# Attention steps spread by weight among the feed-forward steps, from the second H group on

## The chip, the cores and the metric

The kernel runs on one core of one Trainium2 chip. The time is device microseconds of one execution; smaller is better.

## The reference

Two stages, one after the other, over 8 batches of 576 tokens with 8 heads of 64:

```python
scores = scale * np.matmul(q, k.transpose(0, 1, 3, 2))
bias = slopes[:, None, None] * (-np.abs(rel))[None]      # rel = i - j
mask = (rel >= 0) & (rel < 128)
attn = softmax(np.where(mask, scores + bias, -1e9))
x = (attn @ v), heads side by side                       # 4608 x 512
h = x @ w_in                                             # 512 -> 2048
g = h * (1.0 / (1.0 + np.exp(-beta * h)))
out = g @ w_out                                          # 2048 -> 512
```

A row looks back over 128 columns at most, so a block of 128 rows needs its own block of keys and the one before.

## The kernel before

All matmuls are in bf16 with sums in f32. The work is a set of small steps, each a function that issues its instructions on several engines at once.

Attention, for each batch `b`. `TP(b, p)` transposes q and k of head pair `p` on TensorE (eight transposes into two PSUM tiles of `psum_t`, two VectorE copies into `QK`, L230); `TT(b)` does the last 64 rows. Batches from `NTE` = 3 on are transposed by DMA instead (`TD`, L249, on SyncE's queue SP), after a cast on GpSimd (POOL, L129). `SC(b, m, p)` makes scores of a head pair for half the key blocks in one tile of `psum_s`, which has one buffer; for batches 0 and 1 the bias table is added by a matmul and ScalarE takes one exponential (L285), for the later ones ScalarE takes four with a bias (L290) and VectorE multiplies by a mask (L294). `PV(b, qb, g)` multiplies four heads of a row block with the values `VS` (L317, L321) and normalizes on VectorE (L326, L327) into `xn`. `X(b, qb)` transposes `xn` into `XT`: for batches 0 to 2 on TensorE with a copy (L350), for later ones by DMA from SP (L341).

Feed-forward, for each group `g` of 512 tokens (9 groups). `HS(g, j)`, called H below, is four 512-column matmuls (L362), a tanh on ScalarE (`sig`, L367) and a VectorE operation (`gT`, L368); 16 per group. Its PSUM tiles come from `psum_h` (two buffers), in groups 0 and 1 also from `psum_o` (two). `OS(g, i, n)`, called O, is four matmuls (L378); every fourth is followed by a ScalarE evacuation (L384) and, later, a store from POOL.

The order on TensorE is the order in which the program calls the steps. `spread(moe, todo, lead, tail)` walks over the list `moe` of H and O steps and calls after each its share of the attention steps in `todo`, counted by number: none after the first `lead`, all of them before the last `tail`. `merge` puts the loads (`load_qk`, `load_v`), casts, `TD` and the DMA form of `X` (`lazy`) among the steps at due times counted in steps. `by_pair` is the list of a batch that is transposed on TensorE, `by_block` that of a later one.

Before, the stages run so: batch 0 alone; then hs(0), 16 H, with batch 1 spread among them (`lead` 3, `tail` 0); hs(1), 16 H, bare; os(0) and half of os(1), 24 O, with all of batch 2; group 2: hs(2) with the other half of os(1) as H H O eight times, with batch 3 up to the rows that group 3 needs; groups 3 to 8: H of `g` and O of `g - 1` by turns, with the batches' rest; then 16 bare O.

POOL's own queue issues, in an order that the scheduler sets for the early part and the program for the later: the casts of the loaded f32 tiles (`fst`, 13 buffers) of q, k (L113, L119) and v (L141), the loads of W1 and W2, which cast on the way, and from batch 2 on the values (L136), which also cast on the way into `VS`.

## Time and profile before

| | |
|---|---|
| median of 11 runs | 350.56 us (347.57 to 353.08) |
| the profiled execution | 352.3 us, of which its span 350.5 |
| mean granted TensorE clock | 0.984 |
| busy share | TensorE 93%, ScalarE 60%, VectorE 56%, POOL 30% |
| DMA | 138495 packets, 47.67 MB, 125649 of them under 512 B |

A busy share covers stages with quite different limits, so the stages are read one by one: hs(0) with batch 1 runs from 25.6 to 63.3 us, hs(1) from there to 77 us, the 24 O with batch 2 to 109.8 us, group 2 to about 138 us, and the last bare steps from 300 us on. "PEclk" is the clock that TensorE was granted, as a share of full speed. In the views, a releaser behind "<-" is what ended a wait.

### The profile page before, as it was taken

Reading aid. Unit: us, or ns where it says so; the run is one execution under the profiler, and the core shown is the slowest. Engines: PE = TensorE matmul, PEld = TensorE weight load, DVE = VectorE, ACT = ScalarE, POOL = GpSimd, SP = SyncE. Lnnn points to the kernel's source line nnn. Section 1 sums busy time; section 2 is a strip of 40 time slices with the busy share of each in tenths; the row PEclk is TensorE's granted clock in tenths of the full one; section 3 lists DMA queues with packets and bytes.
Section 4 is the critical chain, followed back from the end, with each engine's and each line's share of the span. In section 5 each row is a group of like instructions: output and inputs, shape, how many; then the busy total and the mean of one; then the engine's idle time right before and its main releaser. Section 6 shows DMA issues by size and latency. Waiting matters only on the chain.

```text
span 350.5 us, 6171 instructions
## 1 busy us (share of the span) xinstructions
PE 327.1 (93%) x2279; PEld 154.2 (44%) x2279; DVE 196.9 (56%) x421; ACT 210.9 (60%) x407; POOL 106.8 (30%) x173
## 2 busy tenths in 40 slices
PE   6988969898999789999999999999999999999995
PEld 2454424444454344344454445444544445444442
DVE  6477726776663776566466655665666465334400
ACT  4655843575734895577568756776588654544411
POOL 7639346111574341323225332532000000100000
PEclk9899988999999999999999999999999999999999
DMA  7999999960999999999649995993123002010021
GB/s 206 228 177 251 167 239 232 211 134 21 176 200 178 218 172 167 174 163 153 138 95 177 181 189 138 198 183 68 45 68 61 31 32 67 30 62 30 30 86 66
DMA packets 138495, 47.67 MB, mean 136 GB/s; under 512 B 125649, under 2 KB 135905, under 8 KB 138465
## 3 DMA queue, kind: packets, MB, share of 16 engines
q1 hardware_dynamic: 103520, 31.15, 49.5%
q0 software_dynamic: 34912, 16.13, 34.5%
q8 instruction: 18, 0.29, 0.4%
q14 instruction: 13, 0.10, 0.1%
q10 hardware_dynamic: 32, 0.01, 0.0%
HBM read 36.71 MB, written 9.44 MB: 132 GB/s over the span
## 4 chain that ended last, share of the span: by engine, by line
PE 61%; DMA 13%; issue 9%; ACT 5%; POOL 4%; DVE 4%; SPq 2%; POOLq 0%
PE ops L378 28%; PE hps L362 25%; DMA fst<-in_v_dram 5%; DMA fst<-in_q_dram 4%; ACT pt L290 3%; PE sps L277 3%; PE pv L321 2%; POOL vs L136 2%; DMA fst<-in_k_dram 2%; DMA W<-in_moe_w_in_dram 2%; PE pv L317 2%; SPq L109 1%; DVE gT L368 1%; ACT sig L367 1%; POOL bst L129 1%
## 5 line engine op out<-in xcount | busy, mean ns | idle before, releaser
L367 ACT ACTIVATE sig<-hps,beta_h 128x512 bf16<-128x512 f32 x144 | 99.4, 692 | 80.9 <-PE hps L362 76.6
L362 PE MATMUL hps<-XT,W 128*128 128x512 bf16 x576 | 146.2, 383 | 1.0 <-DVE gT L368 1.0
L378 PE MATMUL ops<-W,gT 128*128 128x512 bf16 x576 | 144.8, 379 | 0.0
L368 DVE SCALAR_TENSOR_TENSOR gT<-sig,hps 128x512 bf16<-128x512 bf16 x144 | 98.3, 684 | 69.5 <-ACT sig L367 69.2
L290 ACT ACTIVATE pt<-sps,bias 128x256 bf16<-128x256 f32 (+1 forms) x192 | 75.1, 479 | 11.9 <-PE sps L277 11.8
L362 PEld LDWEIGHTS <-W 128*128 128x128 bf16 x576 | 52.4, 98 | 60.0 <-issue 4.8
L378 PEld LDWEIGHTS <-gT 128*128 128x128 bf16 x576 | 52.2, 98 | 57.4 <-issue 1.7
L389 POOL DMA_DIRECT2D out_dram<-osb x32 | 17.9, 559 | 171.1 <-ACT osb L384 171.1
L294 DVE TENSOR_TENSOR pt<-pt,mask 128x1024 bf16<-128x1024 bf16 x48 | 35.3, 736 | 24.1 <-ACT pt L290 24.1
L129 POOL CAST bst<-fst 128x512 bf16<-128x512 f32 (+1 forms) x50 | 31.3, 646 | 29.1 <-DMA fst<-in_q_dram 22.7
L384 ACT ACTIVATE osb<-ops 128x512 f32<-128x512 f32 x36 | 21.7, 603 | 26.3 <-PE ops L378 26.3
L327 DVE TENSOR_TENSOR xn<-pv,zs 128x256 bf16<-128x256 f32 (+1 forms) x80 | 33.6, 420 | 2.1
L321 PE MATMUL pv<-vs,pt 128*128 128x65 bf16 x320 | 29.6, 196 | 5.4 <-POOL vs L141 3.3
L326 DVE RECIPROCAL zs<-pv 128x4 f32<-128x4 f32 (+1 forms) x80 | 14.1, 177 | 29.8 <-PE pv L321 29.0
L277 PE MATMUL sps<-qkT 64*128 64x256 bf16 (+2 forms) x320 | 25.6, 255 | 3.8 <-ACT pt L290 3.8
L321 PEld LDWEIGHTS <-pt 128*128 128x128 bf16 x320 | 22.2, 99 | 12.8 <-DVE pt L294 2.7
L317 PE MATMUL pv<-vs,pt 128*128 128x65 bf16 x256 | 24.8, 195 | 1.7 <-DVE xn L327 1.0
L136 POOL DMA_DIRECT2D vs<-in_v_dram x30 | 25.5, 853 | 0.5 <-PE pv L321 0.4
L317 PEld LDWEIGHTS <-pt 128*128 128x128 bf16 x256 | 20.2, 99 | 12.4 <-issue 4.5
L277 PEld LDWEIGHTS <-qkT 64*128 64x128 bf16 x320 | 11.2, 95 | 31.4 <-issue 30.0
L285 ACT ACTIVATE pt<-sps 128x1024 bf16<-128x1024 f32 x16 | 15.9, 1027 | 12.7 <-PE sps L277 12.2
L230 DVE COPY qkT<-tps 128x512 bf16<-128x512 bf16 x24 | 15.5, 684 | 4.0 <-PE tps L226 3.9
(45 smaller groups left out, 104.6 us busy)
## 6 DMA issues: line engine op xcount, KB each, us to landing
fst<-in_q_dram SPq DMA_DIRECT2D x32, 256.0 KB, 4.2
fst<-in_k_dram SPq DMA_DIRECT2D x32, 256.0 KB, 4.8
out_dram<-osb POOLq DMA_DIRECT2D x32, 256.0 KB, 2.8
vs<-in_v_dram POOLq DMA_DIRECT2D x24, 128.0 KB, 5.6
fst<-in_v_dram SPq DMA_DIRECT2D x8, 256.0 KB, 8.0
W<-in_moe_w_in_dram POOLq DMA_DIRECT2D x4, 512.0 KB, 7.7
W<-in_moe_w_out_dram POOLq DMA_DIRECT2D x4, 512.0 KB, 15.2
fst<-in_q_dram SPq DMA_DIRECT2D x8, 128.0 KB, 5.4
```

Of the source, the lines that this page charges most:

```text
L129: nc.gpsimd.tensor_copy(out=t[0 : ROWS[sb], i], in_=f)
L136: nc.gpsimd.dma_start(out=VS[b % 2][0 : ROWS[sb], sb, :, 0:D], in_=v[b, :, P * sb : P * sb + ROWS[sb], :].rearrange("h p d -> p h d"),)
L277: nc.tensor.matmul(o, lhsT=qk[64 * e : 64 * e + 64, 1, p, P * kb : P * kb + P], rhs=qk[64 * e : 64 * e + 64, 0, p, P * kb : P * kb + nq], ...
L290: nc.scalar.activation(out=pt[:, e, cols], in_=sps[:, e, cols], func=ACTF.Exp, scale=qscale, bias=bias[:, half, h : h + 1],)
L294: nc.vector.tensor_tensor(out=pt[:], in0=pt[:], in1=masks[m][:].rearrange("p (o c) -> p o c", o=1).broadcast_to([P, 2, 512]), op=ALU.mult,)
L317: nc.tensor.matmul(pv[:, hl, 0 : D + 1], lhsT=weights(b, qb - 1, h, 1), rhs=vs[:, qb - 1, h, 0 : D + 1], start=True, stop=False,)
L321: nc.tensor.matmul(pv[:, hl, 0 : D + 1], lhsT=weights(b, qb, h, 0), rhs=vs[:, qb, h, 0 : D + 1], start=qb == 0, stop=True,)
L327: nc.vector.tensor_tensor(out=xn[0:nq, 4 * g : 4 * g + 4, :], in0=pv[0:nq, :, 0:D], in1=zs[0:nq].broadcast_to([nq, 4, D]), op=ALU.mult,)
L362: nc.tensor.matmul(hps[:], lhsT=W1[:, c, bass.ts(j, P)], rhs=XT[:, c, c0 : c0 + TOKG], start=(c == 0), stop=(c == NDM - 1),)
L367: nc.scalar.activation(out=sig[:], in_=hps[:], func=ACTF.Tanh, scale=beta_h[:, j : j + 1])
L368: nc.vector.scalar_tensor_tensor(out=gts[g][:, j, :], in0=sig[:], scalar=1.0, in1=hps[:], op0=ALU.add, op1=ALU.mult)
L378: nc.tensor.matmul(ops_[:], lhsT=gT[:, j, i * P : i * P + P], rhs=W2[:, j, :], start=(j == 0), stop=(j == NFF - 1),)
```

## The change

1. `spread` counts by weight: an SC weighs 2, a PV, TP half, TT or TensorE X weighs 1, a DMA X nothing, and a step is called once its weight's share of the slots has passed.
2. `TP` is split in two halves (one PSUM tile each), which are separate steps.
3. hs(0) takes batch 1 without its last block (its two PV and its X), with `tail` 2. The rest of batch 1 and batch 2 up to block 2 are spread over hs(1), os(0) and half of os(1) as one list of 40 steps (`lead` 6, `tail` 7). What is left of batch 2's blocks 3 and 4 goes to the head of batch 3's list.
4. Batch 2's X goes by DMA from SP; batch 1's X is copied by ScalarE instead of VectorE.
5. The loads of batch 2's values are issued after W2's, not as early as the scheduler finds room.
6. Every group from 2 on has the form of the old group 2: H H O eight times with the second half of O of `g - 1`, and then, but for the last, the first half of its own O, eight in a row.
7. `by_block` and the due times in `merge` are altered by a step or two.

The queue of POOL around the loads of batch 2's values (`vs_72` of `in_v`; `vs_73` are batch 1's, `W_79` is W1, `W_80` is W2), before:

```order
L136 DMA vs_72<-in_v_dram 128x8x64
L119 CAST tail_77<-fst 64x512
L136 DMA vs_72<-in_v_dram 128x8x64
L113 CAST bst<-fst 128x512 x2
L136 DMA vs_72<-in_v_dram 128x8x64
L113 CAST bst<-fst 128x512 x2
L189 DMA W_79<-in_moe_w_in_dram 128x4x512
L141 CAST vs_73<-fst 128x8x64
L136 DMA vs_72<-in_v_dram 64x8x64
L141 CAST vs_73<-fst 128x8x64 x3
L192 DMA W_80<-in_moe_w_out_dram 128x4x512 x4
```

and now:

```order
L119 CAST tail_77<-fst 64x512 x2
L113 CAST bst<-fst 128x512 x4
L189 DMA W_79<-in_moe_w_in_dram 128x4x512
L141 CAST vs_73<-fst 128x8x64 x4
L192 DMA W_80<-in_moe_w_out_dram 128x4x512 x4
L141 CAST vs_73<-fst 64x8x64
L113 CAST bst<-fst 128x512 x4
L119 CAST tail_76<-fst 64x512 x2
L113 CAST bst<-fst 128x512 x3
L136 DMA vs_72<-in_v_dram 128x8x64
L113 CAST bst<-fst 128x512
L136 DMA vs_72<-in_v_dram 128x8x64 x3
```

Batch 2's five loads, which stood among the casts of batch 1 and ahead of W1's last part, stand behind W2's and behind casts of batch 2.

VectorE in hs(0), where batch 1's q and k are copied out of the TP tiles (`qkT<-tps`), before:

```order
L368 SCALAR_TENSOR_TENSOR gT<-sig,hps 128x512 x3
L230 COPY qkT_75<-tps 128x512
L368 SCALAR_TENSOR_TENSOR gT<-sig,hps 128x512
L230 COPY qkT_75<-tps 128x512 x3
L368 SCALAR_TENSOR_TENSOR gT<-sig,hps 128x512
L244 COPY qkT_75<-tps 128x8x64
L368 SCALAR_TENSOR_TENSOR gT<-sig,hps 128x512
L230 COPY qkT_75<-tps 128x512 x2
L368 SCALAR_TENSOR_TENSOR gT<-sig,hps 128x512
L230 COPY qkT_75<-tps 128x512 x2
```

and now:

```order
L366 SCALAR_TENSOR_TENSOR gT<-sig,hps 128x512 x3
L229 COPY qkT_75<-tps 128x512
L366 SCALAR_TENSOR_TENSOR gT<-sig,hps 128x512
L229 COPY qkT_75<-tps 128x512
L366 SCALAR_TENSOR_TENSOR gT<-sig,hps 128x512
L229 COPY qkT_75<-tps 128x512 x2
L243 COPY qkT_75<-tps 128x8x64
L366 SCALAR_TENSOR_TENSOR gT<-sig,hps 128x512
L229 COPY qkT_75<-tps 128x512
L366 SCALAR_TENSOR_TENSOR gT<-sig,hps 128x512
```

Three copies stood after one `gT`; now it is one, one, and two with TT's, and the later ones stand alone.

ScalarE at the start of group 2, where four `pt` of 256 (or 320, 192, 320, 192) are one SC and a `sig` is one H, before:

```order
L367 ACTIVATE sig<-hps,beta_h 128x512
L290 ACTIVATE pt<-sps,bias 128x256 x4
L367 ACTIVATE sig<-hps,beta_h 128x512
L290 ACTIVATE pt<-sps,bias 128x256 x8
L367 ACTIVATE sig<-hps,beta_h 128x512 x2
L290 ACTIVATE pt<-sps,bias 128x256 x4
L367 ACTIVATE sig<-hps,beta_h 128x512 x2
L290 ACTIVATE pt<-sps,bias 128x320
L290 ACTIVATE pt<-sps,bias 128x192
L290 ACTIVATE pt<-sps,bias 128x320
L290 ACTIVATE pt<-sps,bias 128x192
```

and now:

```order
L365 ACTIVATE sig<-hps,beta_h 128x512 x3
L289 ACTIVATE pt<-sps,bias 128x256 x4
L365 ACTIVATE sig<-hps,beta_h 128x512 x2
L289 ACTIVATE pt<-sps,bias 128x256 x4
L365 ACTIVATE sig<-hps,beta_h 128x512
L289 ACTIVATE pt<-sps,bias 128x256 x4
L365 ACTIVATE sig<-hps,beta_h 128x512 x2
L382 ACTIVATE osb<-ops 128x512
```

Five SC stood among six H before; now three stand among eight, and no two are neighbours.

The diff, cut to its core:

```diff
     def load_w2(n):
-        nc.gpsimd.dma_start(out=W2[:, bass.ts(n, 4), :], in_=W2v[:, bass.ts(n, 4), :])
+        return nc.gpsimd.dma_start(out=W2[:, bass.ts(n, 4), :], in_=W2v[:, bass.ts(n, 4), :])
...
-    def TP(b, p):
-        src = staged.pop((b, p))
-        for i in range(2):
+    def TP(b, p, i):
+        src = staged[b, p]
...
-        if b >= NTE:
+        if b >= NPE:
             for at, r0, r1 in parts:
                 nc.sync.dma_start_transpose(out=XT[:, :, at : at + r1 - r0], in_=xnv[r0:r1, :])
             return
...
-        copy = nc.vector.tensor_copy if b else nc.scalar.copy
         for at, r0, r1 in parts:
-            copy(out=XT[:, :, at : at + r1 - r0], in_=xt[:, :, r0:r1])
+            nc.scalar.copy(out=XT[:, :, at : at + r1 - r0], in_=xt[:, :, r0:r1])
...
+    cost = {}
+
     def spread(moe, todo, lead=0, tail=3):
-        done, n = 0, len(moe)
+        total, n = sum(cost.get(f, 0) for f in todo), len(moe) - lead - tail
+        done, k = 0, 0
         for i, it in enumerate(moe):
             flush()
             it()
-            to = len(todo) * (i + 1 - lead) // (n - lead - tail)
-            while done < min(len(todo), to):
-                todo[done]()
-                done += 1
+            while k < len(todo) and (i + 1 - lead >= n or (
+                done + cost.get(todo[k], 0)) * n <= total * (i + 1 - lead)):
+                done += cost.get(todo[k], 0)
+                todo[k]()
+                k += 1
+        for f in todo[k:]:
+            f()
+
+    def step(f, c):
+        cost[f] = c
+        return f
+
+    def tp(b, p, i):
+        return step(lambda: TP(b, p, i), 1)
+
+    def tt(b):
+        return step(lambda: TT(b), 1)
 
     def sc(b, m, p):
-        return lambda: SC(b, m, p)
+        return step(lambda: SC(b, m, p), 2)
 
     def pv(b, qb, g):
-        return lambda: PV(b, qb, g)
+        return step(lambda: PV(b, qb, g), 1)
 
     def x(b, qb):
-        f = lambda: X(b, qb)
+        f = step(lambda: X(b, qb), int(b < NPE))
         at[b, qb] = f
-        if b >= NTE:
+        if b >= NPE:
             lazy.append(f)
         return f
 
...
                 t0 = first[b] - 25 + 4.6 * sb
                 jobs.append((t0, lambda b=b, sb=sb, c=casts: c.append(load_qk(b, sb))))
-                jobs.append((t0 + 3.5, lambda c=casts: c.pop()()))
-                jobs.append((t0 + 6.5, lambda b=b, sb=sb: TD(b, sb)))
+                jobs.append((t0 + 4.5, lambda c=casts: c.pop()()))
+                jobs.append((t0 + 8.5, lambda b=b, sb=sb: TD(b, sb)))
                 jobs.append((first[b] - 16 + 3 * sb, lambda b=b, sb=sb: load_v(b, sb)))
         for i, f in enumerate(steps):
             if f in lazy:
-                jobs.append((i + 2.5, f))
+                jobs.append((i + 2, f))
         jobs.sort(key=lambda j: j[0])
         out = []
         for i, f in enumerate(steps):
...
 
     def by_pair(b):
         return [
-            lambda: TP(b, 0), lambda: TP(b, 1), sc(b, 0, 0), lambda: TT(b), sc(b, 0, 1),
-            lambda: TP(b, 2), sc(b, 1, 0), lambda: TP(b, 3), sc(b, 1, 1), pv(b, 0, 0), sc(b, 0, 2),
-            pv(b, 1, 0), sc(b, 1, 2), pv(b, 2, 0), sc(b, 0, 3), pv(b, 3, 0), sc(b, 1, 3),
-            pv(b, 4, 0), pv(b, 0, 1), pv(b, 1, 1), x(b, 0), pv(b, 2, 1), x(b, 1), pv(b, 3, 1),
-            x(b, 2), pv(b, 4, 1), x(b, 3), x(b, 4),
+            tp(b, 0, 0), tp(b, 0, 1), sc(b, 0, 0), tp(b, 1, 0), tp(b, 1, 1), tt(b), sc(b, 0, 1),
+            tp(b, 2, 0), sc(b, 1, 0), tp(b, 2, 1), sc(b, 1, 1), tp(b, 3, 0), pv(b, 0, 0),
+            tp(b, 3, 1), sc(b, 0, 2), pv(b, 1, 0), sc(b, 1, 2), pv(b, 2, 0), sc(b, 0, 3),
+            pv(b, 3, 0), sc(b, 1, 3), pv(b, 0, 1), pv(b, 1, 1), x(b, 0), pv(b, 2, 1), x(b, 1),
+            pv(b, 3, 1), x(b, 2), x(b, 3), pv(b, 4, 0), pv(b, 4, 1), x(b, 4),
         ]
 
     def by_block(b):
 
         e = b - 1
-        r = [pv(e, 2, 1), pv(e, 3, 1), x(e, 2), sc(b, 0, 0), x(e, 3), pv(e, 4, 1), sc(b, 0, 1),
-             x(e, 4)] if e >= NTE else [sc(b, 0, 0), sc(b, 0, 1)]
+        if e < NTE:
+            r = [sc(b, 0, 0), pv(e, 3, 1), x(e, 3), pv(e, 4, 0), sc(b, 0, 1), pv(e, 4, 1), x(e, 4)]
+        else:
+            r = [sc(b, 0, 0), pv(e, 2, 1), x(e, 2), pv(e, 3, 1), x(e, 3), sc(b, 0, 1),
+                 pv(e, 4, 1), x(e, 4)]
         return r + [
-            sc(b, 0, 2), pv(b, 0, 0), sc(b, 0, 3), pv(b, 1, 0),
-            pv(b, 0, 1), sc(b, 1, 0), x(b, 0), pv(b, 1, 1), sc(b, 1, 1), x(b, 1),
-            sc(b, 1, 2), pv(b, 2, 0), sc(b, 1, 3), pv(b, 3, 0), pv(b, 4, 0),
+            sc(b, 0, 2), pv(b, 0, 0), sc(b, 0, 3), pv(b, 1, 0), sc(b, 1, 0), pv(b, 0, 1), x(b, 0),
+            sc(b, 1, 1), pv(b, 1, 1), x(b, 1), sc(b, 1, 2), pv(b, 2, 0), sc(b, 1, 3), pv(b, 3, 0),
+            pv(b, 4, 0),
         ]
 
     with tc.manual_schedule(engines={mybir.EngineType.PE}):
...
-                        load_w2(n)
+                        w2 = load_w2(n)
...
-        steps, first = by_pair(2), {}
+        s1, s2 = by_pair(1), by_pair(2)
+        spread(hs(0), s1[:-3], 3, 2)
+
+        steps, first = s1[-3:] + [f for f in s2[:-3] if f not in (s2[-6], s2[-4])], {}
         for b in range(NTE, B):
             first[b] = len(steps)
             steps += by_block(b)
-        steps += [pv(B - 1, 2, 1), pv(B - 1, 3, 1), x(B - 1, 2), pv(B - 1, 4, 1), x(B - 1, 3),
+        steps += [pv(B - 1, 2, 1), x(B - 1, 2), pv(B - 1, 3, 1), x(B - 1, 3), pv(B - 1, 4, 1),
                   x(B - 1, 4)]
         with tc.manual_schedule(engines={mybir.EngineType.SP, mybir.EngineType.Pool}):
-            for sb in range(NQB):
+            with tc.issue_after(w2.ins):
+                load_v(2, 0)
+            for sb in range(1, NQB):
                 load_v(2, sb)
-            for it in hs(1):
-                it()
             todo, o1, done = merge(steps, first), os(1), 0
             for g in range(1, NTG):
                 if g == 1:
-                    moe = os(0) + o1[0:8]
-                    end = todo.index(at[2, NQB - 1]) + 1
-                elif g == 2:
-                    moe = hs(2)
+                    moe = hs(1) + os(0) + o1[0:8]
+                else:
+
+                    moe, o2 = hs(g), os(g)
                     moe = sum((moe[2 * n : 2 * n + 2] + [o1[8 + n]] for n in range(8)), [])
-                else:
-                    moe = sum(([a, c] for a, c in zip(hs(g), os(g - 1))), [])
-                if g > 1:
-                    end = len(todo)
-                    if g + 1 < NTG:
-                        b, r = divmod(TOKG * (g + 2) - 1, S)
-                        end = todo.index(at[b, r // P]) + 1
-                spread(moe, todo[done:end], 0, 3 if g == 1 else 6)
+                    if g < NTG - 1:
+                        moe += o2[0:8]
+                    o1 = o2
+                end = len(todo)
+                if g + 1 < NTG:
+                    b, r = divmod(TOKG * (g + 2) - 1, S)
+                    end = todo.index(at[b, r // P]) + 1
+                spread(moe, todo[done:end], 6 if g == 1 else 0, 7)
                 done = end
             while stores:
                 flush()
```

More of the change, by code (lines that the diff above doesn't have):

```diff
@@ L219 @@
     pts, xns = {}, {}
-    def TP(b, p):
-        src = staged.pop((b, p))
-        for i in range(2):
-            tps = psum_t.tile([P, LA, P], BF16, name="tps", tag="t")
-            for a in range(LA):
-                nc.tensor.transpose(
-                    out=tps[:, a, :], in_=src[:, i, a, :, :].rearrange("r h d -> r (h d)"),
-                    identity=ident[:],
-                )
-            nc.vector.tensor_copy(
-                out=QK[b % 2][:, i, p, 0:LM].rearrange("c (r a) -> c r a", a=LA),
-                in_=tps[:].rearrange("c a r -> c r a"),
-            )
+    def TP(b, p, i):
+        src = staged[b, p]
+        tps = psum_t.tile([P, LA, P], BF16, name="tps", tag="t")
+        for a in range(LA):
+            nc.tensor.transpose(
+                out=tps[:, a, :], in_=src[:, i, a, :, :].rearrange("r h d -> r (h d)"),
+                identity=ident[:],
+            )
+        nc.vector.tensor_copy(
+            out=QK[b % 2][:, i, p, 0:LM].rearrange("c (r a) -> c r a", a=LA),
+            in_=tps[:].rearrange("c a r -> c r a"),
+        )
     def TT(b):
```

13 lines of the change are left out of this document (8 added, 5 removed).

## The prediction

> **What bounds the kernel now.** I read the page's first two parts first, then the engine's own waits stage by stage, then the stretches where they are longest.
>
> ```profile
> span 350.5 us, 6171 instructions
> PE 327.1 (93%) x2279; PEld 154.2 (44%) x2279; DVE 196.9 (56%) x421; ACT 210.9 (60%) x407; POOL 106.8 (30%) x173
> PE   6988969898999789999999999999999999999995
> PEclk9899988999999999999999999999999999999999
> 63.42 13.92 PE hps L362 x64
> ```
> TensorE is the bound: 93% busy, and no other engine is over 60%. The last row, from the chain of work, shows it at its pace: 64 bare 512-column matmuls in 13.92 us, so a step H (one HS, four matmuls) or O (one OS) costs 13.92 / 16 = 0.87 us. That work cannot shrink here. What can is idle time, lost clock, and small TensorE work. The slices show the holes: near 45 us (the 6) and around 110 us (the 7); slice 5 of the clock row hides a drop that a finer view shows below.
>
> TensorE's own waits, by stretch: 25 to 64 us (hs(0) with batch 1), 64 to 110 (hs(1) bare, then os(0) and half of os(1) with batch 2), 110 to 143 (group 2 and the start of 3), 143 to the end. Columns: total us, times, longest.
> ```profile
> PE pv L321 <- POOL vs L141: 3.3, 2, 2.6
> PE tps L226 <- DVE qkT L230: 1.6, 2, 0.8
> PE xt L345 <- DVE xn L327: 1.0, 1, 1.0
> PE pv L317 <- DVE XT L350: 0.5, 1, 0.5
> ...
> PE sps L277 <- ACT pt L290: 1.2, 4, 0.4
> PE tps L226 <- DVE qkT L230: 1.0, 2, 0.8
> ...
> PE sps L277 <- ACT pt L290: 2.6, 2, 1.7
> PE hps L362 <- DVE gT L368: 1.0, 2, 0.7
> PE pv L321 <- DVE pt L294: 0.7, 2, 0.6
> PE pv L317 <- DVE xn L327: 0.3, 1, 0.3
> ...
> PE pv L321 <- DVE pt L294: 1.3, 3, 0.5
> PE pv L317 <- DVE xn L327: 0.3, 1, 0.3
> ```
> So 6.4 us wait in the first stretch, 2.2 in the second, 4.6 in the third, and only 1.6 in the last 207 us. The largest has a sequel (busy time, then clock, DMA share and GB/s in two stretches; then the two rows of the timeline):
> ```profile
> 45.80:49.20 3.40, 1.46 (x10) 0.62 (x10) 0.35 (x1) 1.65 (x2) 0.01 (x1) 1.00 1.32 230
> 49.20:56.05 6.85, 6.19 (x40) 2.87 (x40) 2.79 (x8) 1.74 (x3) 6.80 (x11) 0.50 1.20 241
> 49.19 0.61 POOL L141 CAST vs<-fst 128x512 bf16<-128x512 f32 x1 [4.14 <-DMA fst<-in_v_dram]
> 49.86 0.21 PE L321 MATMUL pv<-vs,pt 128*128 128x65 bf16 x1 [2.60 <-POOL vs L141]
> ```
> TensorE stood 2.60 us for the fourth row block of batch 1's values, was busy 1.46 us of 3.40, and was then granted half its clock for 6.85 us.
>
> **The values (v wait and clock).** Why were they late? In 30 to 48 us the DMA queues read (packets, MB, share of 16 engines), with two weight loads in 17.5 to 26 us as a price, and the first of the early loads of batch 2's values on POOL:
> ```profile
> q0 software_dynamic: 5736, 1.64, 84.9%
> q1 hardware_dynamic: 5320, 1.93, 59.6%
> ...
> q0 software_dynamic: 1056, 1.05, 79.5%
> W<-in_moe_w_in_dram POOLq DMA_DIRECT2D x2, 512.0 KB, 6.4
> ...
> 27.19 0.89 POOL L136 DMA_DIRECT2D vs<-in_v_dram  x1
> ```
> Two W1 loads take 0.795 x 8.5 = 6.8 us of all engines. The software queue took 0.849 x 18 = 15.3 us in the second window, where two more W1 loads ran, so batch 2's values took about 8.5. Both queues together ran at 1.445, so without them the rest lands some 8.5 / 1.445 = 5.9 us sooner: the cast at 49.19 comes near 43.3. The new order needs it about where the old one did (a slot later, less the transposes' waits): TensorE stood from 47.1. Margin some 3 us. The change holds these five loads behind W2, where they delay nothing early: W2's own loads start sooner by the same shift, and PV of batch 2 first needs them twenty steps H or O (17 us) after hs(1) begins. On POOL they are five issues of 0.89 us that no longer stand ahead of batch 1's casts. Gain: the 3.3 us, and of the half clock 6.85 x 0.5 = 3.4, of which I take 3.2 since 0.66 us of it was idle. Bounds for the pair: 0.7 (the short first wait alone goes) to 6.8.
>
> Here a rule bears on it. The Trainium skill, "TensorE: Matmul & The Clock Gate", section "Why this matters for your kernels", asks for no idle gap over about 3 us. This trace is stricter: 2.60 us idle in a thin stretch sufficed; by the rule alone the clock would not have dropped, and a remaining stop of 2.6 us would cost 2.6 and not 5.8.
>
> **Transposes of batch 1.** Four TPs stood in one slot and waited 1.6 us for the copies out of two buffers; now at most two stand together, with a score step between. Gain 1.5 (bounds 0.5 to 1.6). The waits at the end of batch 1 (1.0 and 0.5) stay: its last X still follows its own PV. ScalarE now copies batch 1's X: nothing, since it was busy only 1.74 us of the 6.85 above. The three steps of batch 1 that go into hs(1) (two PV, one X), and batch 2's last blocks, which go among batch 3's, cost TensorE there what they cost here; nothing but the length of the stretches changes. The later casts and transposes of batches 3 to 7 on POOL and SP I cost at nothing: no wait of TensorE after 60 us in the rows above was ended by a DMA or by POOL; if that cover went, a score step would wait for its transposed q and k.
>
> **X of batch 2.** Five X steps (20 transposes) leave TensorE. In the timeline eight matmuls of a PV go from 57.88 to 58.09, and an X from 58.22 to the next H:
> ```profile
> 57.88 0.19 PE L317 MATMUL pv<-vs,pt 128*128 128x65 bf16 x1 [0.48 <-DVE XT L350]
> ...
> 58.09 0.19 PE L321 MATMUL pv<-vs,pt 128*128 128x65 bf16 x1
> 58.22 0.38 PE L345 MATMUL xt<-ident,xn 128*128 128x128 bf16 x4
> 58.44 0.38 PE L362 MATMUL hps<-XT,W 128*128 128x512 bf16 x1
> XT<-xn SPq DMA_TRANSPOSE x26, 3.1
> ```
> A PV costs 0.24 and an X 0.22 us, so 5 x 0.22 = 1.1 us go. They become five DMA transposes on SP, 3.1 us each to land by the last row, issued one after another; the last three precede hs(2) by seven bare O steps, 7 x 0.87 = 6.1 us, which covers one landing and two more issues. Behind them on SP stand loads of batch 4, wanted two groups later. If that cover failed, hs(2) would start up to 3 us late. Gain 1.1 (bounds -2 to 1.1).
>
> **Group 1.** Batch 2's steps now begin inside hs(1). The units, from the page's groups (count, busy us, mean ns):
> ```profile
> L367 ACT ACTIVATE sig<-hps,beta_h 128x512 bf16<-128x512 f32 x144 | 99.4, 692 | 80.9 <-PE hps L362 76.6
> L368 DVE SCALAR_TENSOR_TENSOR gT<-sig,hps 128x512 bf16<-128x512 bf16 x144 | 98.3, 684 | 69.5 <-ACT sig L367 69.2
> L290 ACT ACTIVATE pt<-sps,bias 128x256 bf16<-128x256 f32 (+1 forms) x192 | 75.1, 479 | 11.9 <-PE sps L277 11.8
> L294 DVE TENSOR_TENSOR pt<-pt,mask 128x1024 bf16<-128x1024 bf16 x48 | 35.3, 736 | 24.1 <-ACT pt L290 24.1
> L384 ACT ACTIVATE osb<-ops 128x512 f32<-128x512 f32 x36 | 21.7, 603 | 26.3 <-PE ops L378 26.3
> L327 DVE TENSOR_TENSOR xn<-pv,zs 128x256 bf16<-128x256 f32 (+1 forms) x80 | 33.6, 420 | 2.1
> L277 PE MATMUL sps<-qkT 64*128 64x256 bf16 (+2 forms) x320 | 25.6, 255 | 3.8 <-ACT pt L290 3.8
> L230 DVE COPY qkT<-tps 128x512 bf16<-128x512 bf16 x24 | 15.5, 684 | 4.0 <-PE tps L226 3.9
> ```
> A score step SC is 25.6 / 64 = 0.4 us of TensorE and 75.1 / 48 = 1.56 of ScalarE. In the last ten H of hs(1) VectorE gets ten gT (6.8), six copies (4.1 at most), two masks (1.5) and two normalizations (0.8 and reciprocals), 13.2 or more; TensorE gets 8.7 of H, five TP and one TT at an X's pace (1.5), two SC (0.8) and 0.7 of batch 1's rest, 11.7. VectorE runs over by 1.5, but H has four PSUM buffers there, two steps or 1.7 us ahead. The old waits (2.2) go; I put 1.7 in their place. Gain 0.5 (bounds -2 to 2.2).
>
> **Groups 2 and on.** Before, group 2 put nine SC into 18 slots with twelve H: ScalarE 12 x 0.69 + 9 x 1.56 + 0.6 = 22.9 us, TensorE 18 x 0.87 + 9 x 0.4 + nine PV at 0.24 = 21.4. ScalarE is over, and 4.6 us were waited. Now each of groups 2 to 7 has some seven SC and nine PV over its 24 first steps with 16 H: ScalarE 11.1 + 10.9 + 1.2 = 23.2, TensorE 20.9 + 2.8 + 2.2 = 25.9. Nowhere over, yet closer (90%) than the old groups from 3 on, which alternate H and O. Two H in a row leave the first one's PSUM buffer 1.7 us until the third H wants it; matmul drain, sigmoid and gT need at least 0.69 + 0.68 and any SC's exponentials stand ahead. I estimate 0.8 us per group, between 1.6 / 5 = 0.3 (the quiet groups) and 4.6 (the old group 2): 6 x 0.8 = 4.8 against 6.2. Gain 1.4 (bounds 4.4 to -21).
>
> Sum: 3.3 + 3.2 + 1.5 + 1.1 + 0.5 + 1.4 = 11.0 us. The profiled execution took 352.3 us, 1.8 over its span and 1.7 over the median of 350.56. So span 339.5, that execution 341.3, and on the median 339.6 us. A difference under 0.5% (1.8 us) can't be told from none.
>
> **The rivals.**
> A. The spread is as quiet in every group as after 143 us: 6 x 0.3 = 1.8 instead of 4.8, and group 1 waits for nothing: 4.7 better, 334.9. For it: the work per slot is now even. Against: pairs of H.
>
> B. The values still come late (the DMA engines stay full: the share is 1.20 even in 49 to 56 us, and W2 moves up into the gap): the wait and the clock drop stay but for 0.7, so 11.0 - 5.8 = 5.2 gained, 345.4.
>
> C. Slower: the pairs of H cost every group what they cost the one stretch where they stand now, 110 to 138:
> ```profile
> 110.00:138.00 28.00, 24.32 (x192) 11.25 (x191) 18.89 (x40) 23.10 (x52) 10.69 (x16) 1.00 1.41 188
> ```
> TensorE was busy 24.32 of 28, 3.7 us idle. Six groups at 3.7 are 22.2 against the 6.2 now: 16 lost, 9.6 gained elsewhere, 357. It decides from (9.6 + 6.2) / 6 = 2.6 us a group. Against it: that stretch also had ScalarE over its time.
>
> D. The short stops add up to a clock drop in each group: once 6.85 us at half clock is 3.4, six times 20.5, against 11.0 gained: 360. The row above speaks against it: with 3.7 us of stops the clock stayed 1.00. This is the rule of the Trainium skill, "TensorE: Matmul & The Clock Gate", section "A second HAM failure mode: psum-queue depth-cycling", by which frequent small idles between matmul groups make the clock oscillate; no stretch here after 60 us shows it.
>
> E. Two of the lower bounds together (B, and hs(2) late for its transposes, and group 1 at -2) leave no difference, near 350.
>
> **How the numbers follow.** Forecast 0.60 (336.5 to 343 by its own bounds), A 0.16, B 0.12, C 0.05, D 0.02, E 0.05. Faster 0.60 + 0.16 + 0.12 = 0.88, same 0.05, slower 0.07. The range 333.5 to 346 takes in the forecast, A and B.
>
> **What would show it.** Right: no wait of PV for the values in hs(0), clock 1.00 from 30 us on, the first bare H of hs(1) some 8 us earlier than 63.4; no rows of X for batch 2; no wait over 1 us of SC for exponentials after 100 us. Wrong: an H waiting for gT many times a group (C), a DMA as what ended an H's wait at a group's start (the X transposes), a low clock after 60 us (D).

## The result, and the profile after

The changed kernel takes 340.69 us (median of 12 runs, 337.44 to 345.4) against 351.05 for the kernel before (47 runs, 347.57 to 354.68): a ratio of 0.9708, 95% interval 0.9676 to 0.974. Medians take in every execution, while a ratio leaves out those that ran over 1.5% longer than the fastest of the same kernel in its series. The forecast was 339.6 with 333.5 to 346, and lies on the same side and within half a per cent. The profiled execution has a span of 338.6 us against 350.5, 11.9 less.

First the page of the changed kernel: its span, the engines, and the slices of TensorE and of its clock.

```profile
span 338.6 us, 6152 instructions
PE 322.1 (95%) x2259; PEld 150.8 (45%) x2259; DVE 193.6 (57%) x411; ACT 212.8 (63%) x412; POOL 107.7 (32%) x173
PE   5999998999989998899999999999999999999995
PEclk9899999999999999999999999999999999999999
```

Busy time fell by 5.0 us (327.1 to 322.1): mainly the transposes that went (1.1) and the half clock, at which the same work takes longer. The rest of the 11.9 was idle time. The 6 and the 7 in the slices are gone.

A span holds much that differs from one execution to the next, so here are stages. Each begins with ScalarE's first `sig` of a group in the timeline, which is the moment the first H of that group is through. The two "again" rows are second profiles of the same two kernels.

| us | to hs(0) | hs(0) | group 1 | groups 2 to end | span |
|---|---|---|---|---|---|
| before | 26.7 | 37.7 | 46.5 | 239.6 | 350.5 |
| before, again | 28.3 | 35.0 | 46.5 | 240.1 | 349.9 |
| after | 26.7 | 28.7 | 45.7 | 237.5 | 338.6 |
| after, again | 28.5 | 28.7 | 44.3 | 239.7 | 341.2 |

The mean of each pair: hs(0) 36.4 to 28.7 (7.7), group 1 46.5 to 45.0 (1.5), the rest 239.9 to 238.6 (1.3); 10.5 in all, and 3% of 351 is 10.3. Seven tenths of the gain lie in the one stretch where batch 1 shares TensorE with hs(0).

There the stop is gone. The stretch of 45 to 50 us after (columns as in the prediction), then the cast that was late:

```profile
45.00:50.00 5.00, 4.48 (x55) 2.51 (x52) 3.69 (x12) 3.84 (x5) 5.00 (x9) 1.00 1.22 220
44.29 0.61 POOL L141 CAST vs<-fst 128x512 bf16<-128x512 f32 x1 [3.52 <-DMA fst<-in_v_dram]
```

The cast of the fourth row block of values starts at 44.29 instead of 49.19 us (the forecast said 43.3), and the clock is 1.00 where it was half. The two rows on H of TensorE's waits over the whole program (total us, times, longest):

```profile
PE hps L360 <- DMA XT<-xn: 4.0, 2, 2.3
...
PE hps L360 <- DVE gT L366: 1.0, 4, 0.3
```

From 26 us on no PV waits for values in that list, and no SC for exponentials. The first row is new and the largest left: an H at the start of a group that waits for a DMA transpose of X, 1.7 us at hs(2) and 2.3 at hs(3). The second row is what the pairs of H wait for `gT`: 1.0 us in seven groups. The kernel before waited 1.0 too, at 138.5 and 142 us, where group 3 begins.

### The profile page after: what moved, and what is told of

The parts are those of the page before. It is cut to its first block, busy times and chain, and to the rows that moved or that the text cites. A ratio compares the mean times of both kernels' runs of the same rounds, so it can differ in the third digit from the quotient of the medians.

```text
span 338.6 us, 6152 instructions
## 1 busy us (share of the span) xinstructions
PE 322.1 (95%) x2259; PEld 150.8 (45%) x2259; DVE 193.6 (57%) x411; ACT 212.8 (63%) x412; POOL 107.7 (32%) x173
## 4 chain that ended last, share of the span: by engine, by line
PE 73%; DVE 8%; DMA 6%; SPq 6%; ACT 4%; issue 2%; POOL 0%
PE hps L360 31%; PE ops L376 28%; PE sps L276 5%; DVE gT L366 3%; ACT pt L289 2%; DMA XT<-xn 2%; PE sps L262 2%; DVE pt L293 2%; PE pv L320 2%; SPq L248 2%; SPq L340 2%; SPq L95 2%; DMA fst<-in_k_dram 2%; PE pv L316 2%; PE tps L225 2%
## 5 line engine op out<-in xcount | busy, mean ns | idle before, releaser
L360 PE MATMUL hps<-XT,W 128*128 128x512 bf16 x576 | 141.0, 379 | 5.7 <-DMA XT<-xn 4.0
L376 PE MATMUL ops<-W,gT 128*128 128x512 bf16 x576 | 137.5, 379 | 0.0
L360 PEld LDWEIGHTS <-W 128*128 128x128 bf16 x576 | 51.4, 97 | 63.3 <-issue 10.3
L129 POOL CAST bst<-fst 128x512 bf16<-128x512 f32 (+1 forms) x50 | 32.1, 656 | 63.7 <-DMA fst<-in_q_dram 43.8
L293 DVE TENSOR_TENSOR pt<-pt,mask 128x1024 bf16<-128x1024 bf16 x48 | 33.8, 705 | 17.6 <-ACT pt L289 16.5
L320 PE MATMUL pv<-vs,pt 128*128 128x65 bf16 x320 | 28.4, 193 | 0.1
L320 PEld LDWEIGHTS <-pt 128*128 128x128 bf16 x320 | 21.6, 97 | 10.1 <-issue 0.2
L316 PE MATMUL pv<-vs,pt 128*128 128x65 bf16 x256 | 24.0, 193 | 1.1 <-DVE xn L326 1.0
L316 PEld LDWEIGHTS <-pt 128*128 128x128 bf16 x256 | 19.9, 98 | 7.9 <-DVE xn L326 1.6
L276 PEld LDWEIGHTS <-qkT 64*128 64x128 bf16 x320 | 10.4, 94 | 28.7 <-issue 26.4
```

What stands on the lines that cost most here:

```text
L129: nc.gpsimd.tensor_copy(out=t[0 : ROWS[sb], i], in_=f)
L276: nc.tensor.matmul(o, lhsT=qk[64 * e : 64 * e + 64, 1, p, P * kb : P * kb + P], rhs=qk[64 * e : 64 * e + 64, 0, p, P * kb : P * kb + nq], ...
L293: nc.vector.tensor_tensor(out=pt[:], in0=pt[:], in1=masks[m][:].rearrange("p (o c) -> p o c", o=1).broadcast_to([P, 2, 512]), op=ALU.mult,)
L316: nc.tensor.matmul(pv[:, hl, 0 : D + 1], lhsT=weights(b, qb - 1, h, 1), rhs=vs[:, qb - 1, h, 0 : D + 1], start=True, stop=False,)
L320: nc.tensor.matmul(pv[:, hl, 0 : D + 1], lhsT=weights(b, qb, h, 0), rhs=vs[:, qb, h, 0 : D + 1], start=qb == 0, stop=True,)
L360: nc.tensor.matmul(hps[:], lhsT=W1[:, c, bass.ts(j, P)], rhs=XT[:, c, c0 : c0 + TOKG], start=(c == 0), stop=(c == NDM - 1),)
```

## The experiments

Each ratio is to the kernel before on the same chip, with its 95% interval. Those of e1, e2, e5 and e10 have three rounds each, those of the rest five.

### e1: the values behind W2, nothing else

On the kernel before, in its old order:

```diff
-            for sb in range(NQB):
+            with tc.issue_after(w2.ins):
+                load_v(2, 0)
+            for sb in range(1, NQB):
                 load_v(2, sb)
```

> The old kernel with one part of the change: batch 2's values are issued behind W2. Theory (early values fill the DMA engines, delay batch 1's, and the stop halves the clock): the wait of PV for values is gone and no half clock after 30 us; the 6.7 us that the changed kernel gained there come at once: ratio 0.981 (344 us). Rival (the DMA engines stay full, so batch 1's values are as late): ratio 0.998 or more, the 2.6 us wait and the half clock still there. The TP waits (1.6 us) stay in both.

Measured: 0.9859 (0.9798 to 0.9921), 4.9 us. In its profile hs(0) takes 32.2 us. The stretch and the cast:

```profile
45.00:50.00 5.00, 5.00 (x54) 2.58 (x52) 2.37 (x8) 3.48 (x5) 5.00 (x9) 1.00 1.22 216
43.87 0.61 POOL L141 CAST vs<-fst 128x512 bf16<-128x512 f32 x1 [3.68 <-DMA fst<-in_v_dram]
```

The same cast comes 5.3 us sooner than in the kernel before and TensorE is busy throughout. The load that it waits for lands 9.8 us after its issue, where it took 13.8 before; that is 4.0 of the 5.3 us, and SP also issued it 1.3 us sooner. So the theory holds: batch 2's values kept batch 1's from landing, through the DMA engines that they share. Rival B, by which the values would stay late, falls. The size is under the 6.5 us of the forecast's two terms; why is told below.

### e2: the new order, the values as early as before

On the kernel after:

```diff
-            with tc.issue_after(w2.ins):
-                load_v(2, 0)
-            for sb in range(1, NQB):
+            for sb in range(NQB):
                 load_v(2, sb)
```

> The changed kernel with the loads of batch 2's values left to the scheduler, as before. Theory: the values of batch 1 are late again, a wait of 2 to 4 us and a half-clock stretch of 6.8 us return in hs(0): 6.5 us slower than the changed kernel, ratio to the old one 0.989 (347 us). Rival (the new order of batch 1's steps alone gives the values time): ratio 0.971 to 0.974, as the changed kernel.

Measured: 0.9695 (0.9631 to 0.9759), no different from the change as a whole. The theory that this queueing carries most of the gain falls, though e1 shows that alone it is worth 1.4%. The stages tell why: hs(0) 31.1, group 1 43.9, the rest 237.4. In hs(0) it loses 2.4 us to the changed kernel, by a stop that is there again:

```profile
48.41 0.19 PE L320 MATMUL pv<-vs,pt 128*128 128x65 bf16 x1 [1.67 <-POOL vs L141]
```

and in group 1 it gets back 1.8 us against the first profile of the change (0.4 against the second): its H waits for X once, at hs(3), and not at hs(2) (its waits, whole program):

```profile
PE hps L360 <- DMA XT<-xn: 2.2, 1, 2.2
```

The delayed loads now share the DMA engines with batch 3's q and k. The issues in 57 to 76 us, with the median us to landing at the end: first the changed kernel,

```profile
vs<-in_v_dram POOLq DMA_DIRECT2D x6, 128.0 KB, 11.7
fst<-in_q_dram SPq DMA_DIRECT2D x2, 256.0 KB, 11.6
...
qkT<-bst SPq DMA_TRANSPOSE x3, 8.2
```

then this one:

```profile
fst<-in_q_dram SPq DMA_DIRECT2D x2, 256.0 KB, 6.7
vs<-in_v_dram POOLq DMA_DIRECT2D x2, 128.0 KB, 4.5
qkT<-bst SPq DMA_TRANSPOSE x3, 3.4
```

Loads and transposes take about twice as long to land where the values stand behind W2. That alone does not make the X at hs(2) late: the second profile of the changed kernel has the same landings (12.0, 11.5 and 8.3 us) and no wait at hs(2). What the two profiles without that wait share is that TensorE comes later to the place, here because hs(0) took 2.4 us longer. The first `sig` of group 2 stands at 101.1 us in the change's first profile, at 101.5 in its second and at 101.6 here, so most of what hs(0) gained by the queueing was lost again at hs(2).

### e10: the stop filled with idle matmuls

On the kernel before: 12 matmuls whose result nothing reads, ahead of the PV that stood 2.60 us, so that TensorE is busy in place of the stop.

```diff
+    def filled(b, qb, g):
+        def f():
+            if b == 1:
+                w = psum_t.tile([P, 512], F32, name="w", tag="t")
+                idle(w[:], 12)
+            PV(b, qb, g)
+        return f
...
-pv(b, 3, 0)
+filled(b, 3, 0)
```

> The old kernel with 12 bare 512-column matmuls on zeros (2.6 us at 0.215) ahead of PV(1,3,0), in the place of the long wait for the values. Theory (the clock drop is a price of its own, behind the wait): the wait is covered by work that is thrown away, the clock stays 1.00, and 3.2 us are gained: ratio 0.991. Rival 1 (at half clock TensorE was not the bound, the drop is free): ratio 1.000. Rival 2 (the fill delays what follows, or the clock falls all the same): ratio 1.000 to 1.007.

Measured: 1.0038 (0.9987 to 1.009), no gain. In its profile the clock of hs(0) is 1.00, and PV waits for values all the same (40 to 60 us):

```profile
PE pv L321 <- POOL vs L141: 3.2, 4, 1.5
```

hs(0) took 37.3 us. The run is inconclusive on the price of half clock: the values came at other times, so that the filled stop was not the only one, and the matmuls take time of their own. The profiled execution took 354.6 us, against a median of 350.83.

### e5: H H O in every group, nothing else

On the kernel before:

```diff
-                elif g == 2:
-                    moe = hs(2)
-                    moe = sum((moe[2 * n : 2 * n + 2] + [o1[8 + n]] for n in range(8)), [])
                 else:
-                    moe = sum(([a, c] for a, c in zip(hs(g), os(g - 1))), [])
+                    moe, o2 = hs(g), os(g)
+                    moe = sum((moe[2 * n : 2 * n + 2] + [o1[8 + n]] for n in range(8)), [])
+                    if g < NTG - 1:
+                        moe += o2[0:8]
+                    o1 = o2
...
-                spread(moe, todo[done:end], 0, 3 if g == 1 else 6)
+                spread(moe, todo[done:end], 0, 3 if g == 1 else 7)
```

> The old kernel with one part of the change: groups 2 and on in the form H H O eight times and eight O of their own, steps still spread by number. Theory (pairs of H cost little, 0.3 to 0.8 us a group, and the longer group 2 is no longer over ScalarE's time): waits after 100 us between 2 and 5 us against 6.2, ratio 0.990 to 1.000, near 0.995. Rival (pairs of H cost each group what they cost the old group 2, 3.7 us): 22 us of waits after 100 us, ratio 1.045.

Measured: 0.999 (0.995 to 1.0031). Groups 2 to the end take 239.2 us, against 239.6 and 240.1 before. So the pairs neither cost nor gain anything that shows, even with steps counted by number, and rival C (3.7 us a group, 1.045) is refuted. H's waits for gT, whole program:

```profile
PE hps L362 <- DVE gT L368: 1.2, 4, 0.4
```

This run shows something else by chance: the same stop in hs(0), nearly as long, without its sequel. The PV in the timeline, then 45 to 50 us:

```profile
49.15 0.19 PE L321 MATMUL pv<-vs,pt 128*128 128x65 bf16 x1 [2.49 <-POOL vs L141]
```

```profile
45.00:50.00 5.00, 2.51 (x22) 1.04 (x22) 0.40 (x2) 1.65 (x2) 1.51 (x3) 1.00 1.27 238
```

TensorE stood 2.49 us and was busy 2.51 of 5, and the clock stayed 1.00, in the next 5 us too. In the 3.40 us from 46.0 on it was busy only 0.91; in the kernel before, a stop of 2.60 us with 1.46 of 3.40 busy cost 6.85 us at half clock.

### e3: batch 2's X back on TensorE

On the kernel after, in X's condition, its weight and the list of the late ones:

```diff
-        if b >= NPE:
+        if b >= NTE:
```

> The changed kernel with batch 2's X back on TensorE (copied by ScalarE), weight 1 each. Theory (hs(2) waits 1.7 us because the last three X stand on SP behind the transposes of batch 3): that wait is gone, 1.1 us of TensorE work comes back, hs(3)'s wait of 2.3 us stays: 0.6 us faster than the changed kernel, ratio to the old one 0.969. Rival (the wait at hs(2) moves to the copies or to the last PV): 1 to 2 us slower, ratio 0.974 to 0.977.

Measured: 0.965 (0.96 to 0.9701), where the change as a whole has 0.9708 (0.9676 to 0.974). Its waits for X and for gT, whole program:

```profile
PE hps L360 <- DVE gT L366: 1.4, 5, 0.5
...
PE hps L360 <- DMA XT<-xn: 0.9, 2, 0.6
```

Group 1 takes 43.9 us against 45.7 and 44.3. The transposes that the change takes off TensorE are no gain: 1.1 us of TensorE were saved, and up to 1.7 at hs(2) waited for it. The intervals overlap, so "better" is not shown; "not worse" is. The expectation missed in one place: the wait at hs(3), which was to stay at 2.3 us, fell to 0.3, though batch 3's X still goes by DMA. With batch 2's X off SP, the X's that hs(3) wants go out there 1.1 us sooner (130.34 against 131.44), and TensorE is done with its bare O 0.7 us later.

### e4: X due sooner on SP

If X lands late, issue it earlier. On the kernel after:

```diff
-                jobs.append((i + 2, f))
+                jobs.append((i + 0.5, f))
```

> The changed kernel with the DMA transposes X due half a step after their place in the list, not two, so that on SP they stand ahead of loads and of q and k's transposes that were due between. Theory (SP is a queue in order; the X of a group's last block is ready and waits behind others): the waits for XT at hs(2) and hs(3), 4.0 us in all, fall under 1.5: 2.5 us faster than the changed kernel, ratio 0.964. Rival 1 (the landing is slow since the DMA engines are full): waits as before, ratio 0.971. Rival 2 (loads now stand behind an X that waits for its xn): SC waits for q and k, ratio 0.975 or more.

Measured: 1.013 (1.0065 to 1.0194): 4.3% slower than the change, slower than the kernel before, and far from what was expected. No SC waits for batch 3's or a later batch's q and k, as Rival 2 has it; it is H that waits. TensorE's waits:

```profile
PE hps L360 <- DMA XT<-xn: 7.2, 2, 4.5
...
PE hps L360 <- issue: 3.7, 1, 3.7
```

The clock falls to half behind each of these three stops, for 6.8, 3.4 and 3.4 us. SP issues in order, and an X that is due before its `xn` is normalized holds up all that stands behind it. In the timeline of SP (start, us):

```profile
86.06 0.63 SPq L95 DMA_DIRECT2D fst<-in_k_dram  x1
...
91.40 1.22 SPq L340 DMA_TRANSPOSE XT<-xn  x1
92.67 0.58 SPq L95 DMA_DIRECT2D fst<-in_q_dram  x1
93.31 1.77 SPq L95 DMA_DIRECT2D fst<-in_k_dram  x1
95.19 2.59 SPq L248 DMA_TRANSPOSE qkT<-bst  x2
97.87 2.73 SPq L340 DMA_TRANSPOSE XT<-xn  x2
```

SP stood 4.7 us (86.7 to 91.4) for one X, and then issued two loads and two transposes of q and k ahead of the X's that hs(2) wanted. The same places in the changed kernel, where the X's that hs(2) and hs(3) waited for are the last row of each piece:

```profile
89.75 3.74 SPq L248 DMA_TRANSPOSE qkT<-bst  x2
93.59 4.66 SPq L340 DMA_TRANSPOSE XT<-xn  x3
...
126.68 2.75 SPq L248 DMA_TRANSPOSE qkT<-bst  x2
129.48 0.57 SPq L95 DMA_DIRECT2D fst<-in_q_dram  x1
130.11 1.22 SPq L95 DMA_DIRECT2D fst<-in_k_dram  x1
131.44 2.65 SPq L340 DMA_TRANSPOSE XT<-xn  x2
```

At hs(2) the last `xn` was begun at 91.39 us, and the seven bare O (28 matmuls) at 92.16:

```profile
91.39 0.42 DVE L326 TENSOR_TENSOR xn<-pv,zs 128x256 bf16<-128x256 f32 x1
92.16 6.22 PE L376 MATMUL ops<-W,gT 128*128 128x512 bf16 x28
```

But the first X of three goes at 93.59, when two transposes of later batches are through. The three land 4.9, 4.8 and 3.0 us after their issue, the last at 99.92, which ends TensorE's wait:

```profile
100.05 1.02 PE L360 MATMUL hps<-XT,W 128*128 128x512 bf16 x4 [1.68 <-DMA XT<-xn]
```

Both orders fail on the same thing, the in-order queue: too late a due time puts prefetches ahead of X, too early a one puts a waiting X ahead of prefetches. Due times between the two were not tried.

### e6: all weights equal

On the kernel after, so that an SC counts as much as a PV:

```diff
-        cost[f] = c
+        cost[f] = min(c, 1)
```

> The changed kernel with every step's weight 1 (a DMA X still 0), so spread by number again. Theory of the prediction (what was over ScalarE's time was the short group 2, not the counting): 0 to 2 us of waits of SC or H come back after 54 us, ratio 0.971 to 0.976. Rival (the weights carry the gain of these groups): SC stand two in a row again, 4 us or more of waits for exponentials, ratio 0.983.

Measured: 0.9829 (0.9761 to 0.9897), so the weights are worth some 1% (1.2% against 0.9708, 0.8 against the 0.9746 of the change's second series, where the intervals touch). The size is the rival's, but its mechanism does not show. No SC of batch 2 or later waits for exponentials; its H's wait for X and for issue. The profiled execution took 353.4 us against a median of 347.3, so these waits are larger than those behind the ratio, and the cause of the 1% is not shown:

```profile
PE hps L360 <- DMA XT<-xn: 7.7, 3, 4.4
PE hps L360 <- issue: 3.8, 1, 3.8
```

With equal weights the list is paced in another way. At hs(3), where the longest wait stands, the last X's go out 1.6 us before TensorE has done its bare O, where it was 2.6 in the changed kernel, so the cover shrinks there. Which step is late first was not followed.

### e8: hs(1) bare again

On the kernel after: `lead` 16 in group 1, so that batch 2 starts with os(0).

```diff
-                spread(moe, todo[done:end], 6 if g == 1 else 0, 7)
+                spread(moe, todo[done:end], 16 if g == 1 else 0, 7)
```

> The changed kernel with the first 16 of the 40 steps of group 1 left bare, so that hs(1) runs alone as before and all of the list falls into 17 slots of O. Theory (spreading over hs(1) buys little, 0.5 us, since VectorE is over its time there): SC waits for exponentials 1 to 2.5 us in the O steps: ratio 0.974 to 0.978. Rival 1 (nothing is lost, hs(1) was as good bare): ratio 0.968 to 0.971. Rival 2 (all that group 1 gained came from it, 2.2 us of old waits and more): ratio 0.980.

Measured: 0.9785 (0.9728 to 0.9841), at the upper end of what was expected; by the ratio alone Rival 2 (0.980) is as near. SC's waits, whole program:

```profile
PE sps L276 <- ACT pt L289: 1.4, 3, 0.5
```

The waits of SC for exponentials are back, 1.4 us, as the theory has it, with as many scores in fewer slots. Group 1 takes 45.1 us, between the change's 45.7 and 44.3. The interval touches that of the change (to 0.974), so between nothing and 1% hangs on the ten slots in hs(1).

### e9: more bare steps at a group's end

The waits for X are a lack of cover at the end of a group, so the cover is made longer: all attention steps are called before the last 10 steps instead of 7, that is 10 x 0.87 = 8.7 us instead of 6.1.

```diff
-                spread(moe, todo[done:end], 6 if g == 1 else 0, 7)
+                spread(moe, todo[done:end], 6 if g == 1 else 0, 10)
```

> The changed kernel with 10 bare steps at the end of each group, not 7 (22 slots for a group's attention instead of 25). Theory (the DMA X of a group's last block, issued behind two loads and two transposes, needs 7 to 8 us, and 7 bare steps are 6.1): with 8.7 us the waits for XT at hs(2) and hs(3), 4.0 us, fall under 1; the denser slots put 1 to 2 us of waits for gT and exponentials in their place: 2 to 3 us faster than the changed kernel, ratio to the old one 0.962 to 0.966. Rival (the denser slots put ScalarE over its time: 22 x 0.87 + 5 = 24.1 of TensorE against 23.2): 4 us or more of SC and H waits, ratio 0.972 or more.

Measured: 0.9612 (0.9571 to 0.9654), 340.35 us on a chip where the kernel before took 352.68 and the unchanged kernel after, in the same series, 343.76. It is faster than the kernel before. Over the change the gain depends on the measure: 1.4% by the ratios, whose intervals are separate, and 1.0% by these medians, though its six executions range from 337.1 to 344.6 us and the change's five from 343.4 to 344.3. From hs(0) to the end its profile takes 310.1 us, against 311.9 and 312.7 in the two of the change, 0.5 to 0.8% less. Its waits:

```profile
PE hps L360 <- DVE gT L366: 1.9, 7, 0.4
...
PE hps L360 <- DMA XT<-xn: 0.7, 1, 0.7
```

X costs 0.7 us instead of 4.0 (or 2.2), and the denser attention, 22 slots for what had 25, waits 1.9 us for `gT` instead of 1.0 (or 1.6).

### e12: both, X on TensorE and a longer tail

e3 with `tail` 9.

> The changed kernel with batch 2's X on TensorE and 9 bare steps at a group's end. Theory: the 0.9 us of waits for XT that are left with batch 2's X on TensorE alone go too, and 0.5 us come back from denser slots: ratio 0.963 to 0.966, the best of all. Rival: the denser slots cost more than the cover saves: 0.968 or more.

Measured: 0.9731 (0.9699 to 0.9763); group 1 45.7 us, the rest 239.4. The two do not add; together they are no better than the change (0.9746 in the same series). An H still waits for X by DMA, which only batches from 3 on have:

```profile
PE hps L360 <- DMA XT<-xn: 1.9, 1, 1.9
```

Batch 2's transposes take TensorE time in denser slots; why the cover that helped in e9 does not help here stays open.

### The two kernels again

> The changed kernel once more, beside the two above on the same chip. If its waits for XT at hs(2) and hs(3) are a matter of the order on SP, they stand there again with 1 to 3 us each; if of chance in the DMA engines' load, elsewhere or not at all. Ratio 0.968 to 0.974.

The unchanged kernel after, in the series of e9 and e12: 0.9746 (0.9715 to 0.9777). Its waits differ from the first profile:

```profile
PE hps L360 <- DMA XT<-xn: 2.2, 1, 2.2
PE hps L360 <- DVE gT L366: 1.6, 6, 0.5
```

One X was late instead of two. At hs(3) the wait is there in both profiles, and in those of e2 and e8 as well (2.2 to 2.3 us). At hs(2) it is gone, though the last X lands at 99.93 us, as in the first profile (99.92): this time hs(0) began 1.8 us later, so TensorE was through with its bare O at 100.4 us and not at 98.4. So it is the queue that sets when X lands, and the sooner TensorE gets there, the longer it stands. At hs(3) the clock dropped this time:

```profile
134.40:137.90 3.50, 1.34 (x8) 0.52 (x7) 0.00 (x0) 0.62 (x2) 2.31 (x4) 1.00 1.14 288
137.90:141.30 3.40, 3.40 (x12) 1.00 (x10) 1.38 (x2) 1.35 (x2) 1.12 (x2) 0.50 1.23 138
```

> The old kernel once more, for a second trace. Theory (a stop of 2.6 us halves the clock only when it falls into one of the clock's own windows of 3.4 us): the wait for the values is there again with 2 to 3 us; the half clock may be there or not; where it is not, hs(0) is 1.5 to 2 us shorter than the 37.8 of the first trace, not 3.2. Rival (every such stop halves the clock, and each half-clock us costs half): the same 37.8.

The unchanged kernel before, one look: 351.66 us. Its PV waited for values 2.6 us (44 to 56 us),

```profile
PE pv L321 <- POOL vs L141: 2.6, 2, 1.4
```

no stop of these was over 1.4 us, the clock of hs(0) stayed 1.00, and hs(0) took 35.0 us instead of 37.7. As the wait fell into two parts, the run does not test what one stop of 2.6 us does.

## Why the forecast came out right, and where its steps were off

**The values: right in mechanism.** Queueing batch 2's five loads behind W2 brought the late cast to 44.29 us (43.3 forecast, from the software queue's share and the price of two W1 loads), the PV's stop went, and the first bare H of hs(1) came at 54.34 instead of 63.35 us: 9.0 us sooner, "some 8" forecast. e1 does it with the one edit.

**The half clock: a term too large.** It was put at 3.2 us, as if every execution paid it. hs(0) less its waits for values is 37.7 - 3.3 = 34.4 us with the drop, and without it 35.0 - 2.6 = 32.4 (before, again) and 36.4 - 3.9 = 32.5 (e5); e1, which has no such wait, takes 32.2. So the drop costs some 2.0 us, as TensorE isn't busy throughout, and one profile in three of that order in hs(0) has it (before; not before again, not e5). If these three are typical it was worth some 0.7 us on the mean.

**The transposes of batch 1: right, and too small.** e1 and the changed kernel have hs(0) without a stop and at full clock, so they differ by the order alone. That stage of e1,

```profile
26.00:58.20 32.20, 28.03 (x253) 14.40 (x252) 22.44 (x50) 19.06 (x24) 18.97 (x31) 1.00 1.19 239
```

and of the changed kernel:

```profile
26.70:55.40 28.70, 26.50 (x233) 13.55 (x232) 19.76 (x41) 21.09 (x28) 17.28 (x28) 1.00 1.20 241
```

TensorE is idle 4.17 us in the first and 2.20 in the second, 2.0 less where 1.5 was forecast. (TP's 1.6 us of waits for the copies went, one of 0.7 for a score step's q and k came, and others shrank. ScalarE's copy of X, put at nothing, ended a wait of 0.8, about what VectorE's had: 0.5 and 0.2.) Its busy time is 1.5 less; of this, batch 1's last three steps, which moved into hs(1), were put at 0.7, and the other 0.8 was not followed. With the values' 3.3 and the drop's 2.0 it makes 8.8 of the 9.0 us between the two first profiles. So that the sum came within 1.1 us of the measured median is in part luck: the drop was charged too high, and this term too low.

**Values and order do not add.** The forecast gave the values 3.3 us of wait as a part of their own. But with the early loads and the new order e2 has 31.1 us in hs(0), 3.9 and 6.6 below the old order's 35.0 and 37.7, and waits for one cast 1.67 us: the order alone hides part of the lateness.

**X of batch 2 on SP: the step that failed.** The forecast said that seven bare O "cover one landing and two more issues", took the gain of 1.1 us, and kept -2 as a bound. The cover did not hold in the first profile: the first X went out 1.4 us after the bare O had begun, behind two transposes of later batches, the last landed 6.3 us after that, and H stood 1.7 us. hs(3) stood 2.3 more for an X that was issued behind two transposes and two loads and landed 4.8 us later, not 3.1; the forecast had put the later transposes on SP at nothing. It looked for what stands behind X on SP, and not for what stands ahead. e9, which does nothing but lengthen the cover, turns 4.0 us of waits for X into 0.7, for a gain of 0.5 to 1.4%.

**Group 1 and groups 2 on: the other sizes.** With the 1.1 for X, group 1 was to gain 1.6 us (0.7 of TensorE's work comes in with batch 1's rest, and as much leaves with batch 2's last three PV), and the groups behind it 1.4 less that 0.7. Measured on the means of two profiles: 1.5 and 1.3. That the sizes are this near is luck, as two errors cancel: the waits for X took 4.0 and 2.2 us that weren't in the sum, and pairs of H cost 1.0 and 1.6 us of waits for gT over seven groups, where 0.8 in each of six, 4.8, was charged. Rival A's premise (0.3 a group) was the right one for the pairs.

**The rivals.** A was half right: quiet groups, but for X. B and C are refuted by e1 and e5. D: the changed kernel's first profile has no clock drop after 11.5 us, and the one in the second follows a single stop of 2.2 us and lasts 3.4 us. The drops that e4, e6, e8 and e10 have after hs(0) also follow one stop each, of 1.66 us or more. That agrees with the row of before and not with the rule of short idles that the prediction weighed against it (the Trainium skill, "TensorE: Matmul & The Clock Gate", section "A second HAM failure mode: psum-queue depth-cycling"): the waits for gT, 0.6 us at most and up to eight a run in the changed kernel and its variants, stand before no drop. E came half true, hs(2) was late, but without B.

**What stays open.** The first late step in e6; why e12 gains nothing; how much of e9's gain is the cover's.

## What to carry to other kernels

A transfer in an in-order queue is as late as what stands ahead of it: price a step that moves to a queue by the issues before it as well as behind, and give it cover at the place where its result is wanted (e9, three more bare steps, 0.5 to 1.4%) rather than an earlier place in the queue (e4, 4.3% lost). An engine that gets there sooner only waits longer for such a transfer. Two remedies for one wait did not add here (e12), so forecast each alone and take the joint gain from the wait. A stop's price in clock is paid in some executions only; compare stages in two profiles of each kernel before a term of 3 us is written down.

## What was not expected of the hardware

Between 1.7 and 2.6 us, whether a stop costs clock is not set by its length. 2.60 us (TensorE busy 1.46 of the 3.40 before the drop) brought half clock for 6.85 us, 2.2 (busy 1.34 of 3.50) for 3.4, and 1.66 in e10 (busy 1.66 of 3.40) for 3.4 too. Yet 2.49 us in e5 (0.91 of 3.40) and 2.34 at hs(3) in the change's first profile (1.06 of 3.40) brought none, and neither did the stop of 1.66 us that the kernel before has at the same score step as e10. The Trainium skill, "TensorE: Matmul & The Clock Gate", section "What's actually happening", has a free-running window of some 3.4 us that decides; the lengths of the drops, 3.4 and twice that, agree with it. But by its rule a window must be idle, and these held over a third of busy time. Where the windows lay in the runs without a drop, no trace shows.

At the start of the program the clock is lost in the same lengths. The first 15 us of the second profile of before, with the clock in the third column from the end, and of e9:

```profile
0.00:15.00 15.00, 10.55 (x59) 4.82 (x62) 7.74 (x21) 5.91 (x16) 10.23 (x24) 0.77 0.91 215
```

```profile
0.00:15.00 15.00, 12.34 (x93) 5.38 (x94) 9.52 (x23) 8.87 (x20) 10.84 (x25) 1.00 0.97 232
```

With the first profile of before between them, at 0.89, these clocks are 6.9, 3.3 and 0 us at half clock, and hs(0) begins at 28.3, 26.7 and 25.2 us: up to 3 us of a span that no edit made, more than the two spans of the changed kernel differ by (338.6 and 341.2). The clock is not all of it: e3 and e8 begin hs(0) at 28.4 and 27.8 us with the clock at 1.00, and their TP wait 2.7 and 2.0 us for casts on POOL in this part, where e9's wait 1.1.
